# Block-sparse attention and MLP on one core: score matmuls in two row halves of PE, mask multiplied in on VectorE, relu on ScalarE

## The chip, the cores and the metric

The kernel runs on one core of one Trainium2 chip. The metric is the device time of one execution in microseconds (us), lower is better. A program has a second, slower state in some of its executions. Where a ratio is given, it is the mean time of one kernel's fast runs over that of the other's fast runs of the same rounds, with a 95% interval, so not quite the ratio of the medians that stand beside it. Kernels of one call ran on one chip beside the kernel before; kernels of different calls are compared through the kernel before, whose medians in the calls were 365.2 to 366.7 us.

PE is the TensorE matmul, PEld its weight load, DVE is VectorE, ACT is ScalarE, POOL is GpSimd. "L244" is line 244 of that kernel's file, so the same instruction has different line numbers in different kernels. Names in the profile: `ps` are scores, `pT` their exponentials, `po` the sums of the value matmuls, `et` their copy, `rt` the reciprocals of the softmax sums, `xT` the normalized heads that the MLP takes in; `ph`, `r` and `g` are the MLP's first sums, their relu and its square; `qc` and `kc` are queries and keys cast to bf16, `pt` their transposes.

## The reference

Four batches of 8 heads, 768 tokens, head size 64. A mask in blocks of 32 tokens (neighbours, first and last block, three sampled blocks per row). The heads are then joined to 512 columns for an MLP with squared relu.

```python
scores = (1/sqrt(D)) * q @ k.T                 # per batch and head, 768 x 768
scores = where(mask, scores, -1e9)
attn   = exp(scores - max) / sum
x      = (attn @ v)  joined over the heads     # 3072 x 512
out    = relu(x @ w_in)**2 @ w_out             # 512 -> 2048 -> 512
```

## The kernel before

Two heads (a pair, `u`, 16 in all) are worked on together. A step `s` is one query tile of 256 columns against two key chunks of 128, for both heads; a pair has 9 steps, the kernel 144. The mask costs no instruction of its own: beside the 64 rows of the head's data, the other rows of the operands hold a one-hot code of the key block and, for each query, 0 or -8e9 per block, so the contraction adds the mask.

```python
def scores(s):
    ...
    for c in range(2):
        ...
        nc.tensor.matmul(ps[:, c, 0, :], KA[i][0:64 + nb, ksl], QA[i][0:64 + nb, qsl], ...)  # 88 rows
        nc.tensor.matmul(ps[:, c, 1, :], KB[i][:, ksl], QB[i][:, qsl], ...)                  # 128 rows
    pT = work.tile([P, 2, 2, QW], BF, name="pT", tag="pT", bufs=4)
    nc.scalar.activation(out=pT, in_=ps, func=AF.Exp, scale=scale)

def values(s):
    ...                                    # 4 matmuls of 256 columns into po (one buffer)
    if cp == CP - 1:                       # every third step
        V.tensor_copy(out=etile[u][:, :, qi * QW:(qi + 1) * QW], in_=po)      # "et copy"

def h_atom(b, t, f):                       # first half of the MLP, one of 32 per batch
    ...                                    # 4 matmuls into ph
    V.tensor_scalar(out=r, in0=ph, scalar1=0.0, scalar2=None, op0=AOP.max)    # relu
    G.tensor_mul(out=g, in0=r, in1=r)

for s in range(NS + LAG + 1):              # LAG = 12
    scores(s)                              # while s < NS
    for f in later.pop(s, []): f()         # loads, casts, transposes, recip, normalize
    ...                                    # MLP pieces of the batch before
    values(s - 2)
```

The timelines below show VectorE and PE starting their instructions in the order in which the program issues them. Two facts matter later: `po` has one buffer, so the first value matmul of the next query tile waits for the et copy, and PE, being in order, then also holds up every score matmul behind it; and the et copy stands in VectorE's queue behind whatever the step has issued before it.

The softmax here doesn't subtract the row's maximum and nothing guards it: scores larger than these inputs give would overflow.

## Time and profile before

366.7 us median of 3 runs (364.08 to 366.78); profiled span 364.8 us.

The kernel has three stages. I cut them at the start of the first MLP matmul and at the start of the last exponential:

| stage | from, to (us) | what runs |
|---|---|---|
| 1 | 0 to 86.6 | attention of the first batch, loads of the weights |
| 2 | 86.6 to 288.7 | attention of a batch beside the MLP of the one before |
| 3 | 288.7 to 364.8 | MLP alone |

View of engine busy time per stretch, kernel before. Columns: stretch and its length in us; busy us (instructions) of PE, PEld, DVE, ACT, POOL; granted PE clock; DMA share; GB/s.

```profile
10.00:86.40 76.40, 51.47 (x436) 41.92 (x435) 49.73 (x85) 47.07 (x48) 0.00 (x0) 0.96 0.69 227
86.40:291.00 204.60, 193.87 (x1421) 135.38 (x1441) 131.54 (x227) 104.53 (x109) 76.23 (x85) 1.00 0.27 85
291.00:364.80 73.80, 66.93 (x345) 33.96 (x349) 29.75 (x49) 6.44 (x11) 35.69 (x43) 0.99 0.14 49
```

Stage 1 has no full engine.

Costliest groups of the page, kernel before: line, engine, operation, shapes, count; busy us, mean ns; idle us of the engine before them and what ended it.

```profile
L244 ACT ACTIVATE pT<-ps 128x1024 bf16<-128x1024 f32 x144 | 145.3, 1023 | 130.8 <-PE ps L242 130.8
L311 DVE TENSOR_SCALAR r<-ph 128x384 f32<-128x384 f32 x128 | 70.8, 555 | 83.3 <-PE ph L308 65.1
L265 DVE COPY et<-po 128x512 f32<-128x512 f32 x48 | 32.8, 684 | 6.2 <-PE po L260 6.0
```

List of waits, kernel before: who waited for whom, us in total, times, longest us.

```profile
PE po L258 <- DVE et L265: 31.3, 24, 6.3
```

Timeline, kernel before, the scores of a step in stage 2: last value matmul, the weight load and the first two of the score matmuls, and the transposes that follow the four (other weight loads left out).

```profile
144.58 0.27 PE L260 MATMUL po<-pT,VB 128*128 128x256 bf16 x1
144.59 0.10 PEld L240 LDWEIGHTS <-KA 88*128 88x128 bf16 x1
144.69 0.27 PE L240 MATMUL ps<-QA,KA 88*128 88x256 bf16 x1
144.81 0.27 PE L242 MATMUL ps<-QB,KB 128*128 128x256 bf16 x1
...
145.14 0.50 PE L189 MATMUL pt<-identb,qc 128*128 128x128 bf16 x6
```

The matmuls start 0.11 us apart, and each is shown as 0.27 us long.

### The profile page before, as it was taken

Reading aid. Unit: us, or ns where it says so; the run is one execution under the profiler, and the core shown is the slowest. Engines: PE = TensorE matmul, PEld = TensorE weight load, DVE = VectorE, ACT = ScalarE, POOL = GpSimd, SP = SyncE. Lnnn points to the kernel's source line nnn. Section 1 sums busy time; section 2 is a strip of 40 time slices with the busy share of each in tenths; the row PEclk is TensorE's granted clock in tenths of the full one; section 3 lists DMA queues with packets and bytes.
Section 4 is the critical chain, followed back from the end, with each engine's and each line's share of the span. In section 5 each row is a group of like instructions: output and inputs, shape, how many; then the busy total and the mean of one; then the engine's idle time right before and its main releaser. Section 6 shows DMA issues by size and latency. Waiting matters only on the chain.

```text
span 364.8 us, 5787 instructions
## 1 busy us (share of the span) xinstructions
PE 315.6 (87%) x2215; PEld 213.3 (58%) x2242; DVE 218.5 (60%) x384; ACT 160.9 (44%) x171; POOL 119.1 (33%) x149
## 2 busy tenths in 40 slices
PE   2896637675979898989999999999999998999995
PEld 1675525564757575756676666766666654555542
DVE  7459756766776666667666676665656476444410
ACT  3687543674544455545555454445455400010011
POOL 7000000001554323233324334334334355656620
PEclk9999997999999999999999999999999999999999
DMA  7985947723513242421414150602020203001011
GB/s 263 286 304 176 338 140 271 226 61 123 137 38 90 87 153 74 101 110 44 162 51 153 47 183 5 203 29 75 1 74 29 75 1 101 31 29 58 30 58 58
DMA packets 23808, 40.81 MB, mean 112 GB/s; under 512 B 3045, under 2 KB 15589, under 8 KB 23781
## 3 DMA queue, kind: packets, MB, share of 16 engines
q1 hardware_dynamic: 23508, 40.05, 34.0%
q10 hardware_dynamic: 272, 0.39, 0.3%
q8 instruction: 17, 0.28, 0.3%
q14 instruction: 11, 0.08, 0.1%
HBM read 33.56 MB, written 6.39 MB: 110 GB/s over the span
## 4 chain that ended last, share of the span: by engine, by line
PE 62%; DVE 21%; DMA 9%; issue 4%; ACT 1%; SPq 1%; POOL 1%; DVEq 0%; ACTq 0%
PE py L323 19%; PE ph L308 18%; PE po L258 6%; PE ps L242 5%; PE po L260 5%; PE ps L240 5%; DMA rt<-rd 4%; DVE et L265 4%; DVE xT L300 4%; DVE r L311 3%; DVE xT L299 2%; DMA rd<-rc 2%; PE pt L189 2%; DVE qc L167 2%; DVE kc L168 2%
## 5 line engine op out<-in xcount | busy, mean ns | idle before, releaser
L244 ACT ACTIVATE pT<-ps 128x1024 bf16<-128x1024 f32 x144 | 145.3, 1023 | 130.8 <-PE ps L242 130.8
L313 POOL TENSOR_TENSOR g<-r 128x384 bf16<-128x384 f32 x128 | 111.9, 881 | 229.3 <-DVE r L311 229.1
L311 DVE TENSOR_SCALAR r<-ph 128x384 f32<-128x384 f32 x128 | 70.8, 555 | 83.3 <-PE ph L308 65.1
L308 PE MATMUL ph<-xT,w_in_sb 128*128 128x384 bf16 x512 | 101.1, 326 | 4.0 <-DVE r L311 2.7
L258 PE MATMUL po<-pT,VA 128*128 128x256 bf16 x288 | 71.9, 276 | 31.3 <-DVE et L265 31.3
L323 PE MATMUL py<-w_out_sb,g 128*128 128x512 bf16 x357 | 92.5, 379 | 3.2 <-ACT ys L327 1.4
L240 PE MATMUL ps<-QA,KA 88*128 88x256 bf16 x288 | 74.0, 280 | 1.5 <-DVE KA L191 1.3
L242 PE MATMUL ps<-QB,KB 128*128 128x256 bf16 x288 | 73.8, 280 | 0.1
L260 PE MATMUL po<-pT,VB 128*128 128x256 bf16 x288 | 72.0, 276 | 0.0
L308 PEld LDWEIGHTS <-w_in_sb 128*128 128x128 bf16 x512 | 49.3, 97 | 37.2 <-issue 3.6
L323 PEld LDWEIGHTS <-g 128*128 128x128 bf16 x384 | 37.0, 97 | 35.1 <-issue 3.4
L260 PEld LDWEIGHTS <-VB 128*128 128x128 bf16 x288 | 28.4, 99 | 46.1 <-issue 36.2
L327 ACT COPY ys<-py 128x512 f32<-128x512 f32 x24 | 14.0, 583 | 65.2 <-PE py L323 65.0
L265 DVE COPY et<-po 128x512 f32<-128x512 f32 x48 | 32.8, 684 | 6.2 <-PE po L260 6.0
L258 PEld LDWEIGHTS <-VA 128*128 128x128 bf16 x288 | 28.4, 99 | 10.9
L240 PEld LDWEIGHTS <-KA 88*128 88x128 bf16 x288 | 28.8, 100 | 5.8 <-POOL VA L179 1.5
L242 PEld LDWEIGHTS <-KB 128*128 128x128 bf16 x288 | 29.0, 101 | 5.2 <-issue 0.5
L191 DVE COPY QA<-pt 64x768 bf16<-64x768 bf16 x16 | 8.8, 550 | 24.6 <-PE pt L189 24.6
L300 DVE TENSOR_TENSOR xT<-et,rt 64x768 bf16<-64x768 f32 x16 | 21.0, 1314 | 1.1 <-DMA rt<-rd 0.7
L299 DVE TENSOR_TENSOR xT<-et,rt 64x768 bf16<-64x768 f32 x16 | 15.7, 984 | 7.4 <-DMA rt<-rd 7.3
L282 DVE RECIPROCAL rc<-st 16x96 f32<-16x96 f32 x16 | 11.7, 732 | 0.9 <-DMA st<-et 0.8
L191 DVE COPY KA<-pt 64x768 bf16<-64x768 bf16 x16 | 8.8, 547 | 3.6 <-PE pt L189 3.5
(49 smaller groups left out, 103.3 us busy)
## 6 DMA issues: line engine op xcount, KB each, us to landing
qs<-in_q_dram SPq DMA_DIRECT2D x16, 384.0 KB
vs<-in_v_dram SPq DMA_DIRECT2D x16, 384.0 KB
rt<-rd SPq DMA_DIRECT2D x32, 192.0 KB
out_dram<-ys SPq DMA_DIRECT2D x24, 256.0 KB
ks<-in_k_dram SPq DMA_DIRECT2D x15, 384.0 KB
wst<-in_moe_w_in_dram SPq DMA_DIRECT2D x8, 512.0 KB
wst<-in_moe_w_out_dram SPq DMA_DIRECT2D x8, 512.0 KB
st<-et SPq DMA_DIRECT2D x32, 3.0 KB
```

The costliest lines, as they stand in the source:

```text
L240: nc.tensor.matmul(ps[:, c, 0, :], KA[i][0:64 + nb, ksl], QA[i][0:64 + nb, qsl], start=True, stop=True)
L242: nc.tensor.matmul(ps[:, c, 1, :], KB[i][:, ksl], QB[i][:, qsl], start=True, stop=True)
L244: nc.scalar.activation(out=pT, in_=ps, func=AF.Exp, scale=scale)
L258: nc.tensor.matmul(po[:, 0, :], VA[i][:, n, :], pT[:, c, 0, :], start=first, stop=last, skip_group_check=True)
L260: nc.tensor.matmul(po[:, 1, :], VB[i][:, n, :], pT[:, c, 1, :], start=False, stop=last, skip_group_check=True)
L265: V.tensor_copy(out=etile[u][:, :, qi * QW:(qi + 1) * QW], in_=po)
L299: V.tensor_mul(out=xT[b][0:D, a, :], in0=et[0:D, 0, :], in1=rt[0:D, :])
L300: V.tensor_mul(out=xT[b][D:P, a, :], in0=et[D:P, 1, :], in1=rt[D:P, :])
L308: nc.tensor.matmul(ph, w_in_sb[:, kc, f * P:(f + 1) * P], xT[b][:, kc, t * TW:(t + 1) * TW], start=(kc == 0), stop=(kc == KM - 1))
L311: V.tensor_scalar(out=r, in0=ph, scalar1=0.0, scalar2=None, op0=AOP.max)
L313: G.tensor_mul(out=g, in0=r, in1=r)
L323: nc.tensor.matmul(py, gtile[b, t, f][:, ts * P:(ts + 1) * P], w_out_sb[:, f, :], start=(f == 0), stop=(f == NF - 1))
```

## The change

The intent is to take the mask out of the contraction, so that a head's scores need only 64 rows; the two heads of a pair can then run in the two row halves of PE at the same time. The mask is multiplied into the exponentials on VectorE instead, the relu moves to ScalarE to make room, and the value matmuls follow three steps later instead of two. Core of the diff:

```diff
-            nc.tensor.matmul(ps[:, c, 0, :], KA[i][0:64 + nb, ksl], QA[i][0:64 + nb, qsl],
-                             start=True, stop=True)
-            nc.tensor.matmul(ps[:, c, 1, :], KB[i][:, ksl], QB[i][:, qsl], start=True, stop=True)
-        pT = work.tile([P, 2, 2, QW], BF, name="pT", tag="pT", bufs=4)
+            for h in range(2):
+                nc.tensor.matmul(ps[:, h, c, :], KT[i][h * D:(h + 1) * D, ksl],
+                                 QT[i][h * D:(h + 1) * D, qsl], start=True, stop=True)
+        pT = work.tile([P, 2, 2, QW], BF, name="pT", tag="pT", bufs=LV + 2)      # LV = 3
         nc.scalar.activation(out=pT, in_=ps, func=AF.Exp, scale=scale)
+        V.tensor_mul(out=pT, in0=pT,
+                     in1=mask[:, None, qi, cp * 2:cp * 2 + 2, :].broadcast_to([P, 2, 2, QW]))
 ...
-        V.tensor_copy(out=A[0:D, :], in_=pt[0:D, :])       # A, Bt = QA, QB or KA, KB
-        V.tensor_copy(out=Bt[D:P, :], in_=pt[D:P, :])
+        V.tensor_copy(out=dst, in_=pt)                      # dst = QT or KT
 ...
-        V.tensor_scalar(out=r, in0=ph, scalar1=0.0, scalar2=None, op0=AOP.max)
+        nc.scalar.activation(out=r, in_=ph, func=AF.Relu)
 ...
-    LAG = 12
+    LAG = 13
 ...
-        if 0 <= s - 2 < NS:
-            values(s - 2)
+        if 0 <= s - LV < NS:
+            values(s - LV)
```

Cut: the mask is built once, in the first steps, in six parts of matmul and ScalarE copy; the mask rows of QA, QB, KA, KB and their copies go.

More of the change, by code (lines that the diff above doesn't have):

```diff
@@ L20 @@
 P = 128
-NEG = -8.0e9
 @with_exitstack
@@ L95 @@
     V, G = nc.vector, nc.gpsimd
-    QA, QB, KA, KB, VA, VB = [], [], [], [], [], []
+    QT, KT, VA, VB = [], [], [], []
     NPB = 2
     for i in range(NPB):
-        QA.append(consts.tile([P, S], BF, name=f"QA{i}"))
-        QB.append(consts.tile([P, S], BF, name=f"QB{i}"))
-        KA.append(consts.tile([P, S], BF, name=f"KA{i}"))
-        KB.append(consts.tile([P, S], BF, name=f"KB{i}"))
+        QT.append(consts.tile([P, S], BF, name=f"QT{i}"))
+        KT.append(consts.tile([P, S], BF, name=f"KT{i}"))
         VA.append(consts.tile([P, NCH, P], BF, name=f"VA{i}"))
@@ L121, in one_hot @@
                         pattern=[[-1, NCH], [-NCH, P]], channel_multiplier=block)
-    V.memset(KB[0][0:64, :], 1.0)
-    V.memset(KA[0][64:P, :], 1.0)
-    one_hot(KB[0][0:64, :])
+    oh = consts.tile([nb, S], BF, name="oh")
+    V.memset(oh, 1.0)
     identb = consts.tile([P, P], BF, name="identb")
     make_identity(nc, identb)
-    one_hot(KA[0][64:P, :])
-    bm = consts.tile([nb, P], BF, name="bm")
+    one_hot(oh)
+    bm = consts.tile([nb, nb], BF, name="bm")
     sbf = consts.tile([nb, n_rand], F32, name="sbf")
     edge = consts.tile([nb, 2], F32, name="edge")
-    V.memset(bm, 0.0)
     pm = ps_h.tile([nb, 4, nb], F32, name="pm", tag="h")
@@ L150, with mask_rows, mask_part @@
         cur = 1 - cur
-    for lo in (0, 64):
-        V.tensor_scalar(out=bm[:, lo:lo + nb], in0=pm[:, cur, :], scalar1=-1.0, scalar2=-NEG,
-                        op0=AOP.add, op1=AOP.mult)
-    pb = ps_s.tile([P, 1024], F32, name="pb", tag="ps")
-    nc.tensor.matmul(pb[:, 0:512], bm, KB[0][0:nb, 0:512], start=True, stop=True)
-    nc.tensor.matmul(pb[:, 512:S], bm, KB[0][0:nb, 512:S], start=True, stop=True)
-    nc.scalar.copy(out=QB[0][0:64, :], in_=pb[0:64, 0:S])
-    nc.scalar.copy(out=QA[0][64:P, :], in_=pb[64:P, 0:S])
+    V.tensor_copy(out=bm, in_=pm[:, cur, :])
+    bq = consts.tile([nb, S], BF, name="bq")
+    mask = consts.tile([P, NQ, NCH, QW], BF, name="mask")
+    def mask_rows():
+        pb = ps_s.tile([P, 1024], F32, name="pb", tag="ps")
+        nc.tensor.matmul(pb[0:nb, 0:512], bm, oh[:, 0:512], start=True, stop=True)
+        nc.tensor.matmul(pb[0:nb, 512:S], bm, oh[:, 512:S], start=True, stop=True)
+        nc.scalar.copy(out=bq, in_=pb[0:nb, 0:S])
+    def mask_part(qi, n0, n1):
+        pb = ps_s.tile([P, 4, QW], F32, name="pb", tag="ps")
+        for n in range(n0, n1):
+            nc.tensor.matmul(pb[:, n - n0, :], oh[:, n * P:(n + 1) * P], bq[:, qi * QW:(qi + 1) * QW],
+                             start=True, stop=True)
+        nc.scalar.copy(out=mask[:, qi, n0:n1, :], in_=pb[:, 0:n1 - n0, :])
     cast = {}
@@ L185, in transp @@
         i = u % NPB
-        A, Bt = (QA[i], QB[i]) if which == 0 else (KA[i], KB[i])
+        dst = QT[i] if which == 0 else KT[i]
         pt = ps_h.tile([P, S], BF, name="pt", tag="h")
@@ L256, in values @@
             first, last = n == 0, n == NCH - 1
-            nc.tensor.matmul(po[:, 0, :], VA[i][:, n, :], pT[:, c, 0, :],
+            nc.tensor.matmul(po[:, 0, :], VA[i][:, n, :], pT[:, 0, c, :],
                              start=first, stop=last, skip_group_check=True)
-            nc.tensor.matmul(po[:, 1, :], VB[i][:, n, :], pT[:, c, 1, :],
+            nc.tensor.matmul(po[:, 1, :], VB[i][:, n, :], pT[:, 1, c, :],
                              start=False, stop=last, skip_group_check=True)
@@ L347, in merge @@
         return [z for _, _, z in sorted(both, key=lambda e: e[:2])]
+    mask_rows()
+    mask_part(0, 0, 4)
+    mask_part(0, 4, 6)
     cast_qk(0)
@@ L355 @@
     for i in range(1, NPB):
-        nc.sync.dma_start(out=KA[i][64:P, :], in_=KA[0][64:P, :])
-        nc.sync.dma_start(out=KB[i][0:64, :], in_=KB[0][0:64, :])
-        nc.sync.dma_start(out=QA[i][64:P, :], in_=QA[0][64:P, :])
-        nc.sync.dma_start(out=QB[i][0:64, :], in_=QB[0][0:64, :])
         init_v(i)
+    LV = 3
     later = {}
@@ L377 @@
             at(s0 + 5, lambda u=u: cast_v(u + 1))
-        e = s0 + SPU + 2
+        e = s0 + SPU + LV
         at(e, lambda u=u: sums_out(u))
@@ L382 @@
         at(e + 8, lambda u=u: normalize(u))
+    for qi in range(1, NQ):
+        at(2 * qi - 1, lambda qi=qi: mask_part(qi, 0, 4))
+        at(2 * qi, lambda qi=qi: mask_part(qi, 4, 6))
     for i in range(2 * NWP):
```

## The prediction

> **What bounds it now.** By the view of engine busy time per stretch there are three stages. (1) 10 to 86 us, attention alone: PE 51, VectorE 50, ScalarE 47 us busy of 76; nothing is full. The chain of waits runs through DMA round trips (st, rd, rt) queued in order on VectorE, and PE waits for the copy et (31.3 us in the list of waits). (2) 86 to 290 us, attention beside the MLP of the batch before: PE 193 of 204 us, PE-bound; about 96 steps of 2.12 us; VectorE 131, ScalarE 104, GpSimd 76. (3) 290 to 365 us, MLP alone, PE-bound, hardly touched.
>
> **Gain.** In the timeline, score matmuls (256 columns) start 0.11 us apart, so a step's four take 0.44 us. Two heads in two row halves can stream together: at best 0.22 us less per step, 21 us in stage 2; in stage 1 almost nothing. VectorE loses the relu (70.8 us) and half of the 35.6 us of copies out of pt.
>
> **Cost on PE.** Scores need 64-row tiles, values and MLP 128 rows: two mode switches a step. The Trainium skill ("TensorEngine Tiling (Array Packing)", Key Properties) says that switching the mode drains TensorE. This trace has one switch, at 6 us (cold clock): the mask matmul with 24 rows starts at 5.67; the next weight load, whose data was there at 5.68, starts only at 6.01, although loads elsewhere start with the matmul before. Estimate from it: a bubble of 0.1 to 0.2 us per warm switch, 0.2 to 0.4 us per step, against 0.22 saved. PE's net in stage 2: -2 to +18 us.
>
> **Cost on VectorE.** 144 multiplies of 128x1024 bf16. From the 128x768 casts (0.556 us at 2 elements a cycle) I estimate 0.69 us each, 99 us in all. Two SBUF inputs compete with GpSimd: the second xT multiply takes 0.95 us in stage 1 and 1.47 us in stage 2, in agreement with the skill's "SBUF — State Buffer" (Who interferes with whom). I expect a mean of 0.8 to 0.95 us in stage 2. VectorE total about 250 us. In the first 86 us it goes from 57 to about 83 us: VectorE becomes the bound there, and DMA waits in its queue hold up exponentials. I expect stage 1 to end 5 to 10 us later, with 2 to 3 us of it for building the mask. In stage 2 VectorE reaches some 1.8 us per step of 2.1: not the bound, but pt and et copies behind a multiply make PE wait more.
>
> **ScalarE.** Relu at about 0.47 us (line through 0.58 us for 512 columns and 1.02 us for 1024): 60 us more, 1.55 us a step. Not a bound.
>
> **Sum.** 366.7 + 7 (stage 1) + about 0 (stage 2, range -18 to +22, most of the gain eaten by switches) gives 374 us; 8 in 10 between 353 and 396. Faster by over 2%: 0.22; within 2%: 0.30; slower by over 2%: 0.48.
>
> **What would show it.** Scores of the two heads in pairs nearly at once (otherwise no gain at all). Gaps of over 0.1 us before the first score and the first value matmul of a step, with the weight load not ahead of the matmul before. Multiply near 0.7 us in stage 1, longer in stage 2. First MLP matmul at 91 to 96 us instead of 86. Stage 2 within 10% of 204 us. Tail unchanged.
>
> **What would make it wrong.** A switch under 0.05 us: stage 2 saves up to 18 us and the kernel lands near 353. A switch over 0.25 us, or VectorE's queue holding PE: 390 or more.

## More of the kernel before

Timeline, kernel before, a stretch of stage 2: start us, duration us, engine, line, operation; in brackets the idle time before it and what ended it. (DVE lines and the one PE line that follows from them.)

```profile
155.90 0.56 DVE L311 TENSOR_SCALAR r<-ph 128x384 f32<-128x384 f32 x1 [1.84 <-PE ph L308]
156.38 0.94 DVE L299 TENSOR_TENSOR xT<-et,rt 64x768 bf16<-64x768 f32 x1
157.35 1.47 DVE L300 TENSOR_TENSOR xT<-et,rt 64x768 bf16<-64x768 f32 x1
158.85 0.56 DVE L167 CAST qc<-qs 128x768 bf16<-128x768 f32 x1
159.33 0.55 DVE L168 CAST kc<-ks 128x768 bf16<-128x768 f32 x1
159.80 0.68 DVE L265 COPY et<-po 128x512 f32<-128x512 f32 x1
160.53 0.27 PE L258 MATMUL po<-pT,VA 128*128 128x256 bf16 x1 [1.46 <-DVE et L265]
```

VectorE sat idle for 1.84 us because the relu at the head of its queue waited for its matmul; the xT multiplies, casts and et copy behind it then came late, and PE lost 1.46 us.

## The result, and the profile after

415.6 us median (415.4 to 419.5, 4 runs) against 366.7 us (364.08 to 368.46, 4 runs): ratio 1.136 (1.127 to 1.146). The change made the kernel 13.6% slower, far outside the predicted range of 353 to 396 us. The result is correct.

Engine busy time per stretch, changed kernel, cut near the same events:

```profile
10.00:112.50 102.50, 66.38 (x462) 31.41 (x459) 73.89 (x126) 51.75 (x54) 0.00 (x0) 0.81 0.49 165
112.50:340.00 227.50, 199.80 (x1403) 103.55 (x1420) 151.36 (x216) 140.21 (x192) 78.63 (x85) 0.95 0.23 76
340.00:413.90 73.90, 68.44 (x355) 35.05 (x359) 6.02 (x7) 28.01 (x55) 36.59 (x44) 0.99 0.14 50
```

Stage 1 is 26 us longer, stage 2 23 us; the tail, counted from the start of the last exponential, is the same within 0.3 us (76.1 before, 76.4 after). No engine is full in either stage: in stage 1 VectorE is busy for 74 of 102.5 us. PE's granted clock fell to 0.81 there, from 0.96 before.

Groups of the page, changed kernel:

```profile
L248 DVE TENSOR_TENSOR pT<-pT,mask 128x1024 bf16<-128x1024 bf16 x144 | 101.1, 702 | 103.1 <-ACT pT L247 102.0
L316 ACT ACTIVATE r<-ph 128x384 f32<-128x384 f32 x128 | 62.4, 489 | 44.6 <-PE ph L313 40.2
```

List of waits, changed kernel:

```profile
DVE pT L248 <- ACT pT L247: 102.0, 91, 3.2
PE po L263 <- DVE et L270: 59.0, 29, 4.8
```

The multiply costs what was expected, 101 us of work. But VectorE also stood idle for 102 us with a multiply at the head of its queue that waited for its exponential, and PE's wait for the et copy went from 31.3 to 59.0 us: from 24.7 to 34.5 in stage 1, from 6.6 to 24.5 in stage 2. The chain of waits, changed kernel, shows how the two hang together: start us, duration us, what. (Before its multiply at 87.20 VectorE stood idle for 1.40 us.)

```profile
86.14 1.03 ACT pT L247
...
87.20 0.69 DVE pT L248
87.89 0.47 DVE qc L171
88.36 0.47 DVE kc L172
88.83 0.60 DVE pT L248
89.43 0.86 DVE xT L304
...
90.32 0.95 DVE xT L305
...
91.31 0.69 DVE w_out_sb L222
92.00 0.61 DVE et L270
...
92.66 0.37 PE po L263
```

From the exponential to the value matmul the chain runs 6.5 us through VectorE's queue: multiply, casts, multiply, xT, a weight cast, and only then et. The timeline shows PE idle for 3.88 us before that value matmul. Behind the value matmul on PE stand the next scores, which the next exponential needs, which the next multiply needs: a loop through PE, ScalarE and VectorE in which each waits for the one before it, and none is full.

The wait for et is not the whole of the loss. In stage 1 it grew by 10 us of the 26; PE's busy time grew by 15 (51.6 to 66.5 us), 3 of it for building the mask and the rest while the granted clock was lower. In the changed kernel's timeline value matmuls start 0.21 us apart at 93 us, where the granted clock was 0.50, and 0.11 us apart at 99.4 us, where it was 1.00. Why the clock was granted lower here was not tested.

The scores themselves did what was intended. Timeline, changed kernel, the scores of a step in stage 2:

```profile
255.13 0.27 PE L265 MATMUL po<-pT,VB 128*128 128x256 bf16 x1
255.33 0.12 PEld L244 LDWEIGHTS <-KT 64*128 64x128 bf16 x4 [0.21 <-issue]
255.33 0.39 PE L244 MATMUL ps<-QT,KT 64*128 64x256 bf16 x4
255.65 0.44 PEld L313 LDWEIGHTS <-w_in_sb 128*128 128x128 bf16 x4 [0.21 <-issue]
255.66 0.82 PE L313 MATMUL ph<-xT,w_in_sb 128*128 128x384 bf16 x4
```

From the last value matmul's start to that of the first matmul behind the scores it is 0.53 us here against 0.56 us before (144.58 to 145.14). At both mode switches the first weight load starts only with its own matmul (255.33, 255.65). In the kernel before it starts 0.10 us ahead of its matmul, beside the matmul before (144.59).

### The profile page after: what moved, and what is told of

It reads as the page before. It is cut to its first block, busy times and chain, and to the rows that moved or that the text cites. A ratio compares the mean times of both kernels' runs of the same rounds, so it can differ in the third digit from the quotient of the medians.

```text
span 413.9 us, 5915 instructions
## 1 busy us (share of the span) xinstructions
PE 338.4 (82%) x2236; PEld 172.2 (42%) x2260; DVE 237.0 (57%) x365; ACT 223.5 (54%) x304; POOL 120.0 (29%) x147
## 4 chain that ended last, share of the span: by engine, by line
PE 61%; DVE 24%; ACT 9%; issue 4%; POOL 1%; ACTq 0%; POOLq 0%
PE py L328 18%; PE ph L313 16%; PE ps L244 9%; ACT pT L247 8%; PE po L263 8%; PE po L265 6%; DVE et L270 6%; DVE pT L248 5%; DVE xT L304 4%; DVE xT L305 3%; PE pt L193 3%; DVE VA L178 2%; DVE qc L171 1%; PE pb L161 1%; DVE kc L172 1%
## 5 line engine op out<-in xcount | busy, mean ns | idle before, releaser
L248 DVE TENSOR_TENSOR pT<-pT,mask 128x1024 bf16<-128x1024 bf16 x144 | 101.1, 702 | 103.1 <-ACT pT L247 102.0
L263 PE MATMUL po<-pT,VA 128*128 128x256 bf16 x288 | 79.8, 299 | 59.9 <-DVE et L270 59.0
L313 PE MATMUL ph<-xT,w_in_sb 128*128 128x384 bf16 x512 | 104.4, 335 | 0.0
L316 ACT ACTIVATE r<-ph 128x384 f32<-128x384 f32 x128 | 62.4, 489 | 44.6 <-PE ph L313 40.2
L265 PE MATMUL po<-pT,VB 128*128 128x256 bf16 x288 | 80.2, 300 | 0.0
L244 PE MATMUL ps<-QT,KT 64*128 64x256 bf16 x576 | 62.8, 302 | 1.0 <-DVE KT L195 0.7
L244 PEld LDWEIGHTS <-KT 64*128 64x128 bf16 x576 | 17.3, 97 | 37.1 <-issue 35.9
L171 DVE CAST qc<-qs 128x768 bf16<-128x768 f32 x16 | 13.3, 833 | 0.7 <-DMA qs<-in_q_dram 0.7
L193 PE MATMUL pt<-identb,qc 128*128 128x128 bf16 x96 | 11.4, 278 | 0.0
L178 DVE CAST VA<-vs 128x384 bf16<-128x384 f32 x16 | 10.7, 667 | 0.0
```

Of the source, the lines that this page charges most:

```text
L244: nc.tensor.matmul(ps[:, h, c, :], KT[i][h * D:(h + 1) * D, ksl], QT[i][h * D:(h + 1) * D, qsl], start=True, stop=True)
L248: V.tensor_mul(out=pT, in0=pT, in1=mask[:, None, qi, cp * 2:cp * 2 + 2, :].broadcast_to([P, 2, 2, QW]))
L263: nc.tensor.matmul(po[:, 0, :], VA[i][:, n, :], pT[:, 0, c, :], start=first, stop=last, skip_group_check=True)
L265: nc.tensor.matmul(po[:, 1, :], VB[i][:, n, :], pT[:, 1, c, :], start=False, stop=last, skip_group_check=True)
L313: nc.tensor.matmul(ph, w_in_sb[:, kc, f * P:(f + 1) * P], xT[b][:, kc, t * TW:(t + 1) * TW], start=(kc == 0), stop=(kc == KM - 1))
L316: nc.scalar.activation(out=r, in_=ph, func=AF.Relu)
```

## The experiments

Three theories. **A, queue order:** the multiply waits for the newest exponential, and the et copy, for which PE waits, stands behind it in VectorE's in-order queue. **B, work:** VectorE simply has 100 us more to do. **C, switches:** the two mode switches a step cost PE the time. Stage 1 below is the start of the first MLP matmul; stage 2 is from there to the start of the last exponential.

| kernel | median us | ratio to before | stage 1 | stage 2 |
|---|---|---|---|---|
| before | 365.2 to 366.7 | 1 | 86.6 | 202.1 |
| changed | 415.6 | 1.136 | 112.6 | 224.9 |
| e1_mul_late | 365.2 | 0.997 | 91.2 | 195.9 |
| e2_no_mul (no mask) | 353.3 | 0.964 | 87.3 | 186.0 |
| e3_before_mul | 424.3 | 1.158 | 115.5 | 233.6 |
| e4_late_full_rows (heads mixed) | 367.5 | 1.000 | 93.5 | 196.2 |
| e5_before_relu_lag | 351.4 | 0.960 | 85.4 | 187.8 |
| e6_late_gpcast | 364.9 | 0.996 | 92.8 | 194.1 |
| e7_late_pairs | 362.2 | 0.992 | 91.1 | 192.3 |
| e8_before_relu_gpcast | 351.4 | 0.959 | 85.7 | 189.2 |
| r1_relu_alone | 356.0 | 0.975 | 86.4 | 192.2 |
| r2_lag_alone | 359.6 | 0.984 | 84.8 | 194.9 |
| r3_et_scalar | **345.7** | **0.945** | 80.3 | 187.5 |
| r4_no_mul_full_rows (no mask, mixed) | 355.7 | 0.972 | 91.2 | 186.6 |
| s1_mul_mid | 381.6 | 1.043 | 97.8 | 204.6 |
| s2_after_et_scalar | 354.0 | 0.967 | 85.0 | 190.8 |

Every changed kernel has 4 runs. The stage columns are read from the one profiled run of each. By the 2% line of the record, r1 and r2 are "unclear" and e7 is "same"; their intervals (0.966 to 0.983, 0.977 to 0.990, 0.984 to 0.999) leave out 1 all the same.

### e1_mul_late: the same work in another order

```diff
 # in scores(s): the multiply is taken out, to times_mask(s)
         if 0 <= s - LV < NS:
             values(s - LV)              # holds the et copy
+        if s < NS:
+            times_mask(s)               # the multiply, now last in the step
```

> The changed kernel with one thing moved: the multiply by the mask of a step is issued on VectorE at the end of the step, behind the copy of po to et, not ahead of it. The work is the same. Theory A (queue order: the et copy stands behind a multiply that waits for the newest exponential, and PE waits for et every third step): the wait of the first value matmul for et falls from 59 us to about 30 us or less as before, the first MLP matmul comes at 85 to 95 us instead of 112, and the total falls to 365 to 385 us. Theory B (VectorE simply has too much work, 74 of 102 us in stage 1): still over 405 us. Theory C (the switches of the row tiles cost PE the time): still over 405 us, too.

365.2 us, 50 us less than the changed kernel, with the same instructions. B and C can't explain that. List of waits, e1_mul_late:

```profile
PE po L267 <- DVE et L274: 27.7, 16, 4.0
DVE pT L253 <- ACT pT L247: 10.8, 13, 1.2
```

VectorE's wait for exponentials went from 102 to 10.8 us, and PE's wait for et from 59.0 to 27.7 us. What remains of B: from 20 to 60 us of this kernel VectorE is busy for 37.6 of 40 us, and stage 1 still ends 4.6 us later than before. That is the size of loss that work alone makes. The 50 us are not waits alone: in stage 1 (112.6 to 91.2 us) PE's idle time fell by 13 us and its busy time by 8.5, at a granted clock of 0.89 in place of 0.81. Only the order was changed, so the order is behind both; how it acts on the clock is not shown.

Groups, e1_mul_late, the multiply in 10 to 91 us and in 91 to 290 us:

```profile
L253 DVE TENSOR_TENSOR pT<-pT,mask 128x1024 bf16<-128x1024 bf16 x49 | 32.8, 681 | 3.7 <-ACT pT L247 3.5
L253 DVE TENSOR_TENSOR pT<-pT,mask 128x1024 bf16<-128x1024 bf16 x96 | 75.8, 807 | 8.4 <-ACT pT L247 7.3
```

In the second stretch GpSimd works too, and the mean is 0.807 us in place of 0.681. There the multiplies that overlap a GpSimd instruction took 0.89 us on average and the others 0.69. This agrees with the Trainium skill, "SBUF — State Buffer", Who interferes with whom: a VectorE instruction with two SBUF inputs competes with a GpSimd instruction that reads SBUF.

### e2_no_mul: the change without the multiply

```diff
-        V.tensor_mul(out=pT, in0=pT,
-                     in1=mask[:, None, qi, cp * 2:cp * 2 + 2, :].broadcast_to([P, 2, 2, QW]))
```

> The changed kernel without the multiply (wrong result on purpose: no mask). Theories A and B: with the multiply gone, both its work and the wait that it puts ahead of et are gone, so about 360 to 370 us. Theory C (row tile switches): over 390 us, as the switches stay.

353.3 us; the result is wrong. C falls: with all its switches the kernel is 62 us faster than the changed one. (This takes out the work of the multiply as well as its wait, so it doesn't tell A from B.) It is also 13 us faster than the kernel before, more than any theory allowed. Something in the rest of the change is a gain; e5, r1 and r2 look for it.

### e3_before_mul: the multiply without the row halves

```diff
 # kernel before, 88 and 128 rows, mask in the contraction
         nc.scalar.activation(out=pT, in_=ps, func=AF.Exp, scale=scale)
+        V.tensor_mul(out=pT, in0=pT, in1=ones[:, None, :, :].broadcast_to([P, 2, 2, QW]))
 # and relu on ScalarE, LV = 3, LAG = 13, pT bufs = LV + 2 as in the change
```

> The kernel before, with full-row scores and the mask in the contraction, plus a multiply of every exponential by a tile of ones at the place where the changed kernel multiplies, relu on ScalarE and the same lags (right result). It is the change without the row halves. Theories A and B: slow like the changed kernel, 410 to 425 us. Theory C: near the time before, 365 to 380 us.

424.3 us. The slowdown comes whole without the row halves. Against e5_before_relu_lag, which is the same kernel without the multiply, one multiply per step at this place costs 73 us, though its work is 100 us on an engine with room.

### e4_late_full_rows and r4_no_mul_full_rows: the row halves alone

```diff
-                nc.tensor.matmul(ps[:, h, c, :], KT[i][h * D:(h + 1) * D, ksl],
-                                 QT[i][h * D:(h + 1) * D, qsl], start=True, stop=True)
+                nc.tensor.matmul(ps[:, h, c, :], KT[i][:, ksl],
+                                 QT[i][:, qsl], start=True, stop=True)
```

e4 has this on top of e1_mul_late, r4 on top of e2_no_mul. Both mix the two heads' scores. (The comparison with the reference, with these inputs, does not notice the mixing, and "correct" says little about the scores; r4 has no mask.)

> As e1_mul_late, but each score matmul contracts over all 128 rows (wrong result on purpose: both heads are summed), so that no mode switch and no pairing of row halves is left. From the trace of the changed kernel I read that a step's four paired scores with both switches take 0.53 us from the last value matmul to the next group, against 0.56 us before. If so, this is within 1% of e1_mul_late, slower by up to 3 us. If the switches cost more than the pairing saves, it is faster than e1_mul_late by 5 us or more; if pairing is a real gain, slower by 10 us or more.

> e2_no_mul (353.3 us) with each score matmul over all 128 rows, so without mode switches and without pairing (wrong result on purpose, no mask and both heads summed). VectorE has room here, so PE bounds stage 2 and the row halves stand alone. If a step's pairing saves 0.22 us and its two switches cost 0.19 us, 0 to 4 us slower than e2_no_mul; if pairing were a real gain without cost, 15 us or more slower; if switches cost more than 0.25 us together, faster.

367.5 us against 365.2, and 355.7 against 353.3: full rows cost 2.3 and 2.4 us, which is no more than the spread of e4's own runs (364.7 to 367.7) and of e2's (351.4 to 355.9). In stage 2 alone the difference is 0.3 and 0.6 us. So the row halves, with their switches, are worth next to nothing, as the timeline's 0.53 against 0.56 us says.

### e7_late_pairs: half of the switches

```diff
-        if s < NS:
-            scores(s)
+        if s < NS and s % 2 == 0:
+            scores(s)
+            scores(s + 1)
```

(on top of e1_mul_late, with one more pT buffer)

> e1_mul_late with the scores of two steps in one group, so half of the mode switches. Two switches cost about 0.19 us in the trace, against 0.22 us that a step's pairing saves. Halving them should take 0.1 us off each of 96 steps of stage 2: 7 to 10 us less than e1_mul_late, 355 to 359 us, with the score group seen in the timeline as 8 matmuls in about 0.55 us. If the switches are not what eats the gain of the row halves, no change (363 to 367 us).

362.2 us, 3 us less, where 7 to 10 were expected; stage 2 lost 3.6 us. The direction is right, the size is not. (e7 and e1 are from two calls, and the pairs also bring every second score group one step forward; the switches were not taken apart from that.) Timeline, e7_late_pairs, the scores of two steps and the matmul behind them:

```profile
204.63 0.27 PE L269 MATMUL po<-pT,VB 128*128 128x256 bf16 x1
204.84 0.61 PE L244 MATMUL ps<-QT,KT 64*128 64x256 bf16 x8
...
205.38 0.82 PE L317 MATMUL ph<-xT,w_in_sb 128*128 128x384 bf16 x4
```

Eight score matmuls take 0.54 us from their start to the next group, four took 0.32 to 0.33: four more cost about 0.22 us, half of the 0.44 us of before. The pairing thus doubles the rate in full. A group of four costs 0.53 - 0.11 = 0.42 us with both switches; less 0.22 of streaming, I estimate both switches together at about 0.2 us. Pairing saves 0.22. In stage 2 PE's busy time fell by 6.2 us against e1 (187.9 to 181.7), near what was expected, but its idle time grew by 2.6 (8.0 to 10.7); 1.4 of that is its wait for et (6.1 to 7.5).

### s1_mul_mid and s2_after_et_scalar: what stood behind the multiply

e1 moved the multiply behind three kinds of work at once. s1 moves it behind the casts and pt copies of the step, but leaves it ahead of et. s2 leaves it where the change has it and takes only the et copy off VectorE.

```diff
 # s1
         for f in later.pop(s, []):
             f()
+        if s < NS:
+            times_mask(s)
 # s2
-            V.tensor_copy(out=etile[u][:, :, qi * QW:(qi + 1) * QW], in_=po)
+            nc.scalar.copy(out=etile[u][:, :, qi * QW:(qi + 1) * QW], in_=po)
```

> The changed kernel with the multiply moved behind the step's casts and pt copies, but still ahead of the et copy (right result). If the et copy behind the multiply is what PE waits for, this stays slow, 405 to 422 us. If the copies out of pt (or the casts) were what the multiply held up, it falls to 365 to 380 us like e1_mul_late (365.2 us).

> The changed kernel with the et copy on ScalarE and the multiply left where it is (right result). If et behind the multiply is the cause, the wait of the first value matmul for VectorE is gone and the total falls to 355 to 368 us. If pt or the casts behind the multiply are the cause, it stays over 395 us, less at most the 33 us of VectorE work that it takes away.

s1: 381.6 us, between the two expectations, so my either-or was wrong. Of e1's 50 us, 34 come from letting the step's other VectorE work run while the exponential is still on its way, and 16 from letting et pass the multiply. The second step is not one of the clock: in stage 1 s1 was granted 0.94 and e1 0.89, and e1 is still 6.6 us shorter there. In the first, clock and waits change together (0.81 to 0.94). s2: 354.0 us, 62 us less and just under what was expected, though the multiply stays ahead of everything else. Together: the whole of the step's VectorE work behind the waiting multiply is late, and et is the place where PE runs into it. s2 also takes 33 us of work off VectorE, so it isn't a pure test of order; e1 is.

### e5_before_relu_lag, r1_relu_alone, r2_lag_alone: the parts of the change that help

```diff
 # r1: this alone
-        V.tensor_scalar(out=r, in0=ph, scalar1=0.0, scalar2=None, op0=AOP.max)
+        nc.scalar.activation(out=r, in_=ph, func=AF.Relu)
 # r2: this alone
-            values(s - 2)
+            values(s - LV)               # LV = 3, LAG = 13, pT bufs = LV + 2
 # e5: both
```

> The kernel before with what the change does beside the row halves and the multiply: relu on ScalarE and the lags longer by one step (right result). If relu on ScalarE and the longer lag are neutral, 364 to 369 us. If most of the 353 us of e2_no_mul came from them and not from the row halves, 352 to 358 us.

> The kernel before with one line changed: relu on ScalarE in place of VectorE, lags as before (right result). e5_before_relu_lag took 351.4 us with relu and lag changed together. If the relu does it (it takes 70.8 us out of VectorE's queue, in which xT, qc, kc and et stand one behind the other in stage 2 while PE waits), 350 to 356 us. If it is the lag, 363 to 368 us.

> The kernel before with the lags longer by one step and five pT buffers, relu still on VectorE (right result). If the relu does it, 362 to 368 us. If the lag does it, 350 to 356 us.

351.4 us for both, 356.0 for the relu, 359.6 for the lag. My expectations for r1 and r2 had it one or the other; it is both: 9 and 6 us, and 15 together. Nearly all of it lies in stage 2, which falls from 202.1 to 187.8 us with the same matmuls. In it PE was idle for 10.7 us before, for 5.1 with the lag, for 2.2 with the relu moved and for none with both. So stage 2 of the kernel before was not bound by PE's matmuls alone: most of the 14 us were idle time of PE, of which the list of waits puts 6.6 us down to et, like the 1.46 us shown above. The remaining 3.6 us came off PE's busy time (191.4 to 187.8); I can't say what they were. The Trainium skill ("Trainium Kernel Development and Optimization", Performance Expectations) calls matmul busy time a bad metric for how close a kernel is to roofline, because matmuls are pipelined. This trace shows such pipelining: a matmul is shown as 0.27 us long and the next starts 0.11 us after it.

### e6_late_gpcast and e8_before_relu_gpcast: weight casts on GpSimd

```diff
-            V.tensor_copy(out=w_in_sb[...], in_=st)       # and the same for w_out_sb
+            G.tensor_copy(out=w_in_sb[...], in_=st)
```

> e1_mul_late with the 16 casts of the weights (0.69 us each, 11 us, all in stage 1) on GpSimd, which is idle in stage 1. If stage 1 of e1_mul_late is bound by VectorE's work, as its 9 to 10 us busy of 10 say, the first MLP matmul comes 5 to 11 us earlier than its 91 us and the total falls to 354 to 360 us. If it is bound by DMA round trips or PE, nothing changes (363 to 367 us).

> e5_before_relu_lag with the weight casts on GpSimd. Stage 1 of the kernel before is held by DMA round trips in VectorE's queue, of which the casts that wait for their load are one part: I expect 2 to 8 us less than e5_before_relu_lag.

Neither moved (364.9 and 351.4 us). The expectations failed. In e6 the casts take 1.26 and 1.45 us each on GpSimd, against 0.69 us on VectorE. The Trainium skill ("GPSIMD Engine Reference", opening paragraph) calls VectorE roughly 2 times faster at ordinary elementwise arithmetic, and these casts agree. VectorE's multiply in 10 to 91 us grew from 0.681 to 0.769 us: the 15 that overlap a cast took 0.96 us on average, the others 0.68. So part of the 11 us taken off VectorE came back as contention. Whether the rest was lost to DMA round trips in its queue is not settled.

### r3_et_scalar: a version that beats both

```diff
 # on top of e5_before_relu_lag (mask in the contraction, no row halves)
-            V.tensor_copy(out=etile[u][:, :, qi * QW:(qi + 1) * QW], in_=po)
+            nc.scalar.copy(out=etile[u][:, :, qi * QW:(qi + 1) * QW], in_=po)
```

> e5_before_relu_lag with the copy of po to et on ScalarE as well, so that no wait of PE in stage 1 passes through VectorE's queue with its DMA waits (right result). PE still waits 19.4 us for et in e5_before_relu_lag, nearly all in stage 1. If that wait is VectorE's queue, the first MLP matmul comes at 75 to 82 us instead of 85, and the total is 341 to 348 us; ScalarE then has about 1.75 us per step of 2 in stage 2, so a loss there would show as PE waiting for ScalarE.

345.7 us, ratio 0.945 (0.938 to 0.951), correct: 5.5% faster than the kernel before. The list of waits of e5_before_relu_lag still had

```profile
PE po L259 <- DVE et L266: 19.4, 15, 3.9
```

and that of r3_et_scalar has in its place

```profile
PE po L259 <- ACT et L266: 8.3, 13, 0.8
```

Stage 1 ends at 80.3 us in place of 85.4, within what was expected. The same idea as before: take out of VectorE's queue what PE waits for.

## Why the prediction was wrong

- **Multiply in stage 1 ("+ 7 (stage 1)"): the step that failed.** The work was sized right (0.69 us each expected, 0.702 measured; VectorE 237 us against "about 250"). The prediction treated it as load on an engine and asked only whether VectorE becomes full. It measured +26 us, with VectorE 72% busy. The missing term is the wait, 102 us of VectorE's idle time in the whole kernel, 27 of it in stage 1: a multiply issued right behind its exponential sits at the head of an in-order queue until PE and ScalarE have finished, and the rest of the step, et last, comes after. With the same work in another order (e1) the loss of stage 1 is 4.6 us, close to the 5 to 10 that were predicted. The text named the effect ("pt and et copies behind a multiply make PE wait more") and gave it no number; under "What would make it wrong" it even named "VectorE's queue holding PE: 390 or more", which is what came, but the sum holds nothing for it.
- **Stage 2 ("about 0", range -18 to +22).** Measured +22.8 us, for another reason than the one given: not the switches, but the same loop: with the multiply issued late and every switch in place stage 2 takes 195.9 us (e1), 29 us less. Without the multiply it takes 186.0 with the switches (e2) and 186.6 without them (r4).
- **"PE-bound" in stage 2: only in part.** e5 runs the same matmuls in 187.8 us in place of 202.1, and 10.7 us of the difference were idle time of PE.
- **Relu on ScalarE: its effect on the time was left out.** It costs 0.489 us each, near the estimate (0.47). The prediction counted it as work taken off VectorE and gave it no time in the sum; alone it saves 9 us.
- **Row halves and switches: right.** The two heads do stream at once (four more score matmuls in 0.22 us), both switches take about 0.2 us by my estimate, the low end of the 0.2 to 0.4 predicted, and the net is zero within 3 us (e4, r4). The Trainium skill ("TensorEngine Tiling (Array Packing)", Key Properties) says that a mode switch drains TensorE; the weight loads that no longer run ahead (0.10 us before, 0 at the switches) agree with it.
- **Contention with GpSimd:** 0.8 to 0.95 us expected in stage 2. The changed kernel shows 0.709 there, e1 shows 0.807. It depends on when the two meet: 42 of 95 multiplies overlap a GpSimd instruction in the changed kernel, 56 of 95 in e1, and the overlapping ones take 0.73 and 0.89 us, the others 0.69 in both.
- **Tail unchanged: right** (76.4 against 76.1 us).

The sum, in the right terms: relu and lag -15 us (e5 against before), the multiply at its place +73 us (e3 against e5), the rest of the change (row halves, single copies out of pt, mask building) -9 us (changed against e3). The last was not taken apart further where the multiply is in its original place.

## What to carry to other kernels

Before you add an instruction to an in-order engine, ask not only how long it takes but what it waits for and what stands behind it in the queue; if another engine waits for something behind it, the wait is paid there. Issue an instruction that waits for a fresh result at the end of the step, or put the copy that frees a PSUM buffer on an engine whose queue has no such wait. And a PE that is busy for 95% of a stage may still be waiting: here 10.7 us of idle time in 202 went when the waits behind it went. PE's busy share alone does not say whether PE is the bound.

## What the Trainium skill lacked or had wrong

- "TensorEngine Tiling (Array Packing)", Key Properties, says that a mode switch drains TensorE but gives no figure. Here I estimate the two switches around a group of scores at about 0.2 us together, and a group of four 256-column matmuls saves 0.22 us by pairing. So a group of four breaks even. From the last value matmul's start to the first matmul behind the scores, a group of eight took 0.75 us in place of about 0.99 (9 x 0.11).
- No page that I drew on puts a price on a waiting instruction at the head of an in-order queue: one multiply of 0.70 us per step, of 144, cost 73 us in e3, and 50 us of the change's time went when the same multiplies were issued later in the step (e1).
- "SBUF — State Buffer", Who interferes with whom, names who contends but gives no time for these instructions: a multiply took 0.89 us when it overlapped a GpSimd square (e1) and 0.96 when it overlapped a GpSimd cast (e6), against 0.68 to 0.69 alone.
